# Chunk 2's normed rows take another way into the MLP, in a newly ordered DeltaNet + MLP kernel

## The chip, the cores and the metric

The kernel runs on one core of a Trainium2 chip. The metric is the device time of one execution in microseconds (us). The core has five engines that each run their own instruction stream in order: TensorE (PE; PEld is its weight load), VectorE (DVE), ScalarE (ACT), GpSimd (POOL) and SyncE (SP), which only issues DMAs here. Engines wait for each other by semaphores.

## The reference

A DeltaNet attention over 4 batches, 8 heads, 768 positions and head size 48 is followed by an MLP block on the rows of 8 x 48 = 384 values:

```python
for t in range(S):
    y[:, :, t] = einsum('bhd,bhde->bhe', q[:, :, t], state)
    v_old = einsum('bhde,bhd->bhe', state, k_n[:, :, t])
    state = state + beta_t * einsum('bhd,bhe->bhde', k_n[:, :, t], v[:, :, t] - v_old)
x = y as (B, S, H*D)
xn = (x - mean) / sqrt(var + 1e-6) * g_ln
out = x + relu(xn @ w_ch1) @ w_ch2          # 384 -> 1536 -> 384
```

Keys are divided by their norm first. All of it is float32.

## The kernel before

The 768 positions are cut into 12 chunks of 64. A chunk holds 4 x 64 = 256 rows for the MLP. The names c0 to c11 stand for the recurrence of a chunk (`recur`, from L1020) and m0 to m11 for its MLP (`mlp`, from L1420).

For a chunk's recurrence the kernel needs a Gram matrix of its keys (`gram`, stored to DRAM in `gds`), the inverse of a triangular matrix made from it, products with queries and state, and the state's update. From chunk 2 on the inverse is made for two chunks together: `rows_inverse` (L864) loads blocks of the Gram matrices from DRAM, eliminates column by column on VectorE (L906 and L913, 31 columns) and stores the result to DRAM, from where it is loaded back as blocks (`xq`). `join` (L964) joins the blocks on TensorE.

At the end of `recur` stands the path of the rows into the MLP, which the change touches. ScalarE copies the attention's output to `x` (L1164). VectorE takes mean and variance (L1170, L1171), ScalarE the root (L1176), VectorE the normed rows `xln`, one instruction of 128 rows for each of two row groups (L1182). The MLP needs them turned, with the 384 channels on partitions, scaled by `g_ln`: the tile `xnt`. There are two ways to it, and the constant `LNPE` chooses by the chunk's number:

- `c <= LNPE`: for each row group TensorE turns three blocks of 128 x 128 into a PSUM bank (L1216, tile `by`, or `two` in chunk 0), and ScalarE (or VectorE, L1221) scales them into `xnt`, 128 columns at a time (L1231).
- `c > LNPE`: VectorE turns blocks of 32 x 32 into `xlt` (L1193, one instruction a row group), SyncE stores `xlt` to the DRAM tile `xld` (L1198) and loads it back with four DMAs, one for each 32 partitions (L1201), and ScalarE scales three times 256 columns (L1208). In this way the columns of `xnt` come in another order, which alternates blocks of 32 rows of the two row groups.

The MLP of chunks 0 to 2 is written out plainly: 12 tiles of the first layer (L1438 for chunk 0, L1458 for chunks 1 and 2), a ReLU on ScalarE (L1446, L1467). From chunk 3 on (`FROM`) the first layer is `fifteen`, which makes it from sums of blocks (L1339; it needs the columns alternated). The second layer is plain in chunk 0 (L1480) and `seven` from chunk 1 on (L1555), with 42 products of 128 x 192. In chunks 1 and 2 the ReLU writes `h_all` with the two row groups apart:

```python
h_all[:, hk] if c <= LNPE else h_all[:, hk].rearrange("p (g i b) -> p i g b", g=2, b=BK),
p[:, 0:TOK] if c <= LNPE else p[:, 0:TOK].rearrange("p (i g b) -> p i g b", g=2, b=BK), ACTF.Relu,
```

The order of the work is written out by hand. Every function only records steps (`Line.add`): an engine, a closure that issues one or several instructions, and what it reads and writes. The string `ORDER` (L131 to L242) lists all steps by number, and `Line.emit` issues them in that order; `in_this_order` then holds every engine to it, so that an engine's stream is the listed steps of that engine, one after the other. SyncE's DMAs stand in the same list: one that waits for its data holds up those behind it. The letter f stands for a filler, a product of zeros on TensorE (L1633) that keeps it busy. They stand in the first 60 us, where chunk 0's inverse is made by a chain of short steps on TensorE, VectorE and ScalarE (`first_inverse`).

Weights arrive as pairs of 32-bit words and are put together by ScalarE, VectorE and GpSimd (`convert`) in the first 110 us, from DMAs that ScalarE issues.

Of the kernel before, what the change touches and what calls it, by code (L numbers as in the profile page):

```python
# [131 lines left out]
52 59 57 54 58 56 8 10 9 11 5 12-13 2 0 65 15 14 41 49 254 66 43 7 19 23 1 45 47 46 48 53 55 6 39 72 37-38 76 71 69 89  # L132
96 f 79-80 f f 85-86 81-82 105-106 88 90-91 87 103-104 17 31 16 20 97 92-93 83 74 98 84 107 99 73 70 75 40 108 213 26
18 35 21-22 100-101 94 34 102 95 24 124-125 118 219 211 78 128 f f f f 109-110 f f f 220 126 29 119 32 120 111 122 112
129 77 123 121 225 127 223 241 113 63-64 67 261 312 263 260 259 256 258 262 257 323 313 408 405 68 311 310 f 130 132
131 133 f f 140 134 f f 224 141-142 135-136 215 143 138-139 137 145 235 221 144 245 229 227 212 247 243 253 226 42 61
f f f 146 f f 147 4 f 148 150 114 149 156 f 152 242 25 33 28 151 246 f 155 161 154 153 f f f 115 162 f 659 62 60 658
44 661 f 157 236 27 158 163 166-167 116-117 159-160 244 248 360 164 206 f f 264 171 169-170 f 265 30 165 228 266 36
267 168 3 268 255 269-273 50 216 172 178 361 175-176 233 177 231 217 51 179 f f f 207 182 174 173 274-277 184 278 183
208 214 367 237 187 185-186 180 f f 325 403 398 324 322 238 663 181 209 279-280 f 314 316 366 194 188 281 195 282  # L140
189-190 362 240 283 232 284-298 363 299-300 f 315 317 198 193 199 239 201 318-319 200 191-192 f 320 f f f 368 210 196
326-327 334 197 202 364 335 338 329 203 249 204 328 340 342-343 205 251 346 671 230 234 218 670 664-665 222 369
347-348 f f f 330 336 f 352 f 331-332 355 353-354 673 250 252 672 365 674 662 660 572 337 339 358 573 341 344-345
349-351 574 576 407 409 402 321 410 301 406 399 356-357 304-306 411 333 400 309 303 302 308 307 472 474 471 473 404
359 432 431 788 401 415 575 370 578 598 434 433 579 412 577 435 580-581 675 470 413 582 584 599 372 585 604 373 605
583 475 588 610 586 611 587 416 378 589 379 616 592 617 417 593 596-597 635 418 590 636 591 594 666 436 371 414 437
602 374 384 595 600 382 603 376 608 601 609 385 790-792 794 793 787 789 784 476-479 481 677 482-499 419-420 500-502
480 375 503-504 439 421 1075-1076 676 377 614 422 424 615 606 425 391 423 607 380 390 620 438 426 430 427 429 428 386
505-507 678 508-513 1087 381 514-524 383 1088 621-623 612 440-441 637 624 638 392 442 394 388 443 445 447 446 613 387
795 525 393 444 389 395 1086 396-397 1089-1090 1077 639 625 667 450 448 668 526 650 527-534 449 535-537 626-627  # L150
679-680 452 451 453 538-539 628 640 796 651 454 641 629 618 630 656 652 455-457 653-654 540 657 541-544 458 642 631
462 459-460 465 619 463 643-647 797 632 921 785 1181 929 922-924 669 930 681 931 684 683 686 685 786 1079 682 1078 655
545 1183 648-649 933 926 549 546-547 464 461 826-827 687-691 693-708 548 634 928 1180 934-935 932 830 832 828 833 831
838 836 798 839 837 842 829 843 834 844 835 845 799 850 853 851 1091 1074 468 1081 1093 852 857 854 466 1080 467 1092
800 709-714 550 692 715-722 551 723-724 561 725 936 726-730 859-863 554 552-553 555-560 840 864 801 841 865 802 876
846 867 856 866 805 807 806 803 562 877 848 878-879 810 808 811 809 804 847 564 815 812 563 813 816 731 849 565 817
822 814 818 825 566 821 819-820 823 869-873 824 927 567 570 569 568 571 732 1082 733-740 937 940-941 938 942 939 1553
1098 883 855 880 886-887 881 888-889 874 943 858 868 469 1555 1186 1188-1189 1187 925 1190 1371 633 1179 1191 944 1369
1178 1370 741 875 742-745 890-891 746-756 892 894-899 757 945-946 1185 1661 1374 1192 947 882 948 901-903 1083 893 885
949 951-952 1084 955 1094 1184 1554 884 1375 904 979 905-907 900 980 977 909 974 1565 1095-1096 950 953 956 985 981  # L160
1193 954 986 982 958 912-914 1194 915-917 975 959-960 976 1197 962 918 1198 971 1003 978 972-973 908 1085 758 760 1097
761 759 1102 1100-1101 1099 991 983 987 1377 1182 1378 1195 762 957 961 763 992 984 764-765 767 1103 988 766 997 989
768 990 1004 1006 1567 1556-1557 773 1196 769-771 998 772 995 993 1200 1012 994 996 1001 1104-1107 1109-1121 1199 1201
1002 1202 1013 1022 1014 999-1000 1015-1017 1023 1203 774 920 1379 910 919 963 1380 964 1373 966 1381 967 911 1376 965
1853 1007 1005 1010 1008-1009 1569 1552 1558 1011 1021 1568 1019-1020 1559 1564 1018 1029 1024-1025 1030 1039-1042
1031 1043 1032 1026-1027 1044 1033 1566 1037 970 969 968 1383 1852 1382 1036 1243 1236 1122-1139 1045 1028 1140-1141
1034 1046 1228 1038 1232 1054 1229-1230 1233 1247 1047-1052 1035 1204 1560 1053 1384 1205 1055-1059 775 778 777 1207
1206 1208-1209 1142 1210-1211 1385 776 779 782 1215 783 1212 781 780 1388 1060 1065-1069 1240 1070 1237 1231 1386 1389
1216 1143 1387 1390 1144 1213 1145 1217 1214 1146-1148 1391-1392 1238 1241 1248-1249 2045 1571 1570 1251 1255 1234
1071 1218 1149 1219 1393 1239 1252 1244 1253 1245 1254 1246 1256 1242 1150-1151 1250 1372 1855 1854 1656 1660 1664  # L170
1658 1657 1666 1663 1072 1665 1667 1220 1668 1062 1279 1270 1221 1224 1669 1223 1073 1222 1394 1267 1257 1264 1268
1265 1258 1572 1395 1108 1266 1561 1235 1289 1271 1284 1061 1259 1269 1152-1153 1275 1154-1161 1562 1272-1273 1276
1274 1277 1260 1280 1162-1163 1278 1573-1574 1281 1285 1261 1290 1286 1291 1164 1282 1165-1168 1292 1563 1063 1670
1169-1172 2152 1575 1064 1173 1283 1227 1293 1317 1396 1294-1295 1262 1318-1319 1296 1307-1309 1320 1310 1226 1225
1263 1297 1311-1312 1287 1313 1288 1321-1322 1324-1325 2047 2057 1577 1579 1578 1176 1580 1177 1174 1671 1326-1329
1323 1330 1298 1419 1299 1301 1304 1300 1302 1426 1305 1314-1315 1430 1303 1306 1316 1334-1336 1423 1342-1344 1420
1337-1339 1175 1851 1858 1850 1860 2150 1859 2153 1345-1346 1340 1349 1347-1348 1350-1352 1331 1360 1421 1353 1662
1332 1341 1581-1583 1398 1397 1584-1585 2058 1576 1587 1462 1333 1588 1424 1438 1354-1355 1357 1586 1401 1399-1400
1361-1362 1427-1428 1363-1365 1439 1434 1356 2044 1672-1673 1422 1403 1366 1589 1431 1435-1436 1425 1590-1595 1402
1596 1674 1429 1675-1676 1437 1677 1432 1440-1441 2059 1472 1453-1454 1467 2046 2049 2048 2056 2051 2061 1678 1597  # L180
1433 1442 1598 1447-1448 1450 1455 1680 1406 1682 1679 1681 1449 1683 1451 1456 1443-1444 1458 1407 1599-1602 1404
1603 1405 1604-1605 1684 1452 1606 1445 1686 1457 1459-1460 1463-1464 1468 1473-1474 1465 1461 1466 1469 1685 1408
1475 1687 1409 1476 1490-1491 1477-1478 1689 1856 1688 1410 1690 1481-1482 1484 2050 1483 1488 1470 1446 1471
1492-1495 1500-1503 1498 1607 1479-1480 1485 1487 1497 1608-1609 1504-1505 1359 1610 1486 1489 1499 1691 1496 1862
1857 1861 1863 1368 1659 1358 1506 1864 1411 1367 1414 1611-1613 1507-1510 1525 1511-1513 1614-1615 1866 1517-1522
1526 1523 1616-1617 1694 1692 1514 1524 1413 1412 1415 1417 1695 1618 2052 1619-1620 1693 2148-2149 2151 2345 1418
1416 1532-1534 1527-1531 1535-1536 1696 1717 1515 1724 2060 1718 1867 1728 1516 1697-1700 1865 2155-2156 2158
1543-1546 1537 1621-1625 1869 1868 1870-1872 1874 1547 1873 1876 1704 1701 1875 1548 1721 1719 1722 1538 1626
1725-1726 1627-1629 1705-1706 1630 1702 1720 1727 2062 1736 1732 2063 1737 1760 1877 1723 1549 1631 1880 1878 1708
# [56 lines left out]
def kernel(  # L246
# [18 lines left out]
    DFF = w_ch1.shape[1]  # L265
    KC = DM // 128
    FT = DFF // 128
    GH = 2 * H
    NP = H // 2
    TURNED = 4  # L270
    LNPE = 2
    GP = 2 * NP
    FROM, LATER = 3, 6
    JOINT = 3
    TOK = 256
    WN = 768

# [1504 lines left out]
```

## Time and profile before

| | us |
|---|---|
| median of 3 runs | 515.05 |
| lowest and highest | 513.08, 516.33 |
| profiled execution, its own time | 514.4 |
| its span | 512.7 |
| busy: TensorE | 499.4 |
| VectorE | 355.0 |
| GpSimd | 281.7 |
| ScalarE | 208.0 |

The span runs from the first to the last instruction of the profile; 1.7 us of the execution lie around it. Busy time is the union of an engine's instructions; an engine that is not busy waits or has nothing to do. TensorE's matmuls are pipelined, so rows that follow each other overlap a little, and each float32 product shows as two rows. The granted clock of TensorE is 0.997 on the mean. The chain of work that ended last is read from the end: at each step to what released the instruction, or to the one before it on its engine.

### The profile page before, as it was taken

The page shows a single profiled execution, that of the slowest core. Times are in us where ns is not written, and L with a number is a line of the kernel's source. Part 1 is how long each engine was busy: PE and PEld are TensorE (multiplying, and loading weights), DVE is VectorE, ACT ScalarE, POOL GpSimd, SP SyncE. Part 2 cuts the span into 40 slices and gives each one's busy share as a digit, 9 for nine tenths or more (in the row PEclk, how much of TensorE's full clock was granted, in tenths as well). Part 3 has the DMA queues.
Part 4 walks back from the last instruction along what each step waited for, and adds up shares of the span by engine and source line. Part 5 has one row for each costly group of instructions (what it writes and reads, how often), then busy time and mean ns, then how long its engine had stood idle before and what let it go on. Part 6 is the DMA issues. An engine that isn't in the chain of part 4 may idle for free.

```text
span 512.7 us, 21868 instructions
## 1 busy us (share of the span) xinstructions
PE 499.4 (97%) x9490; PEld 455.4 (89%) x9490; DVE 355.0 (69%) x843; ACT 208.0 (41%) x462; POOL 281.7 (55%) x447
## 2 busy tenths in 40 slices
PE   7998998999999999999999999999999999999997
PEld 5786897668898889899999999999999999999996
DVE  5677469698896798984989957998935555353241
ACT  4877644532443342251435243424323424324140
POOL 5442872344667879749574456264282732745554
PEclk9999899999999999999999999999999999999999
DMA  8979685578339756387433483442472303012011
GB/s 202 266 145 217 119 180 123 115 176 168 43 56 217 151 98 106 67 214 125 88 90 55 92 219 60 102 72 50 99 138 39 91 3 95 3 40 54 2 40 31
DMA packets 181631, 54.49 MB, mean 106 GB/s; under 512 B 164888, under 2 KB 177312, under 8 KB 181536
## 3 DMA queue, kind: packets, MB, share of 16 engines
q1 hardware_dynamic: 168512, 40.10, 37.7%
q10 hardware_dynamic: 10816, 9.83, 6.9%
q0 software_dynamic: 2208, 3.17, 4.2%
q8 instruction: 74, 1.21, 1.0%
q14 instruction: 21, 0.17, 0.1%
HBM read 36.30 MB, written 16.78 MB: 104 GB/s over the span
## 4 chain that ended last, share of the span: by engine, by line
PE 90%; DVE 4%; issue 2%; DMA 2%; ACT 1%; SPq 1%; POOL 0%; POOLq 0%; DVEq 0%; ACTq 0%
PE f L1555 28%; PE f L1339 23%; PE f L1458 6%; PE f L1633 4%; PE f L1480 3%; PE f L1438 3%; PE by L1031 2%; PE two L818 2%; PE two L1047 2%; PE by L1126 2%; PE two L1119 2%; PE two L1136 2%; DMA words<-in_moe_w_ch_dram 1%; PE by L980 1%; PE f L616 1%
## 5 line engine op out<-in xcount | busy, mean ns | idle before, releaser
L1542 POOL TENSOR_TENSOR h_all<-h_all 128x256 f32<-128x256 f32 x99 | 72.2, 741 | 18.7 <-DVE qt L913 4.6
L1555 PE MATMUL f<-w_sb,h_all 128*128 128x192 f32 x396 | 80.8, 331 | 0.0
L1555 PE MATMUL f<-words,h_all 128*128 128x192 f32 x396 | 75.8, 328 | 0.0
L1580 POOL TENSOR_TENSOR words<-h_all 128x128 f32<-128x128 f32 x66 | 30.0, 474 | 66.3 <-ACT h_all L1366 51.1
L1555 PEld LDWEIGHTS f<-w_sb,h_all 128*128 128x128 f32 x396 | 64.4, 190 | 1.8 <-DVE o L1573 0.2
L1362 DVE TENSOR_TENSOR h_all<-f,h_all 128x512 f32<-128x512 f32 x72 | 48.7, 684 | 24.7 <-PE f L1339 17.1
L1555 PEld LDWEIGHTS f<-words,h_all 128*128 128x128 f32 x396 | 64.9, 190 | 0.7
L906 DVE TENSOR_TENSOR tmp<-xb,gb 128x31 f32<-128x31 f32 (+19 forms) x139 | 52.4, 377 | 4.0 <-POOL xb L893 0.4
L1357 ACT COPY h_all<-f 128x512 f32<-128x512 f32 x45 | 26.0, 585 | 67.0 <-PE f L1339 60.7
L913 DVE TENSOR_TENSOR xb<-xb,tmp 128x31 f32<-128x31 f32 (+19 forms) x139 | 49.0, 352 | 3.3
L400 POOL DMA_DIRECT2D tb<-in_k_dram x64 | 42.2, 663 | 9.4 <-DMA ksum<-gd 9.1
L1366 ACT ACTIVATE h_all<-h_all 128x512 f32<-128x512 f32 x54 | 32.4, 626 | 28.3 <-DVE h_all L1362 28.1
L1339 PE MATMUL f<-xnt,w_sb 128*128 128x128 f32 x288 | 41.2, 279 | 0.0
L1339 PE MATMUL f<-x_new,w_sb 128*128 128x128 f32 x288 | 39.8, 277 | 0.0
L1339 PEld LDWEIGHTS f<-xnt,w_sb 128*128 128x128 f32 x288 | 36.9, 191 | 0.7
L1339 PEld LDWEIGHTS f<-x_new,w_sb 128*128 128x128 f32 x288 | 36.4, 192 | 0.7 <-DVE h_all L1362 0.2
L1573 DVE TENSOR_TENSOR o<-f,x 128x192 f32<-128x192 f32 x33 | 11.5, 351 | 33.5 <-PE f L1555 28.6
L1164 ACT COPY x<-by 128x384 f32<-128x384 f32 x23 | 10.5, 481 | 57.2 <-DVE o L1573 32.8
L1458 PE MATMUL f<-xnt,w_sb 128*128 128x256 f32 x144 | 33.6, 383 | 0.0
L1458 PEld LDWEIGHTS f<-xnt,w_sb 128*128 128x128 f32 x144 | 26.8, 190 | 3.6
L1633 PE MATMUL f<-u 128*128 128x256 f32 x94 | 26.1, 411 | 2.8 <-DVE xb L448 2.8
L681 POOL TENSOR_TENSOR v<-v,kpair 128x768 f32<-128x768 f32 x10 | 14.9, 1486 | 23.5 <-DVE xln L1182 13.7
(259 smaller groups left out, 1048.2 us busy)
## 6 DMA issues: line engine op xcount, KB each, us to landing
words<-in_moe_w_ch_dram ACTq DMA_DIRECT2D x20, 384.0 KB, 6.2
gd<-gsb SPq DMA_DIRECT2D x11, 512.0 KB, 4.4
v<-in_v_dram SPq DMA_DIRECT2D x24, 192.0 KB, 4.4
kr<-in_k_dram SPq DMA_DIRECT2D x46, 96.0 KB, 3.6
out_dram<-o SPq DMA_DIRECT2D x46, 96.0 KB, 2.4
xld<-xlt SPq DMA_DIRECT2D x9, 384.0 KB, 3.6
xnt<-xld SPq DMA_DIRECT2D x36, 96.0 KB, 2.8
tb<-in_q_dram SPq DMA_DIRECT2D x40, 64.0 KB, 3.0
```

The lines of the kernel that those rows point to most:

```text
L400: add(eng, cost, lambda: QUEUE[eng].dma_start(out=out_, in_=in_), r, w, bulk=n * ns / 16e3, np=n, **kw)
L906: lambda j=j, n=n, w=w, t=t: nc.vector.tensor_tensor(out=t, in0=xv[:, 0:n, j : j + 1].to_broadcast([128, n, w]), in1=gv[:, j : j + 1, j + ...
L913: "DVE", dve(n * w), lambda t=t, rest=rest: nc.vector.tensor_tensor(out=rest, in0=rest, in1=t, op=ALU.subtract),
L1339: nc.tensor.matmul(wide(p[:, f : f + 128]), w[:, f : f + 128], r, start=start and i == 0, stop=True, skip_group_check=True)
L1357: add("ACT", act(512), lambda: nc.scalar.copy(o, p), pk, ok)
L1362: add("DVE", dve(512), lambda: nc.vector.tensor_tensor(out=o, in0=x, in1=y, op=op), [*xk_, *yk], ok)
L1366: add("ACT", act(512), lambda: nc.scalar.activation(o, o, ACTF.Relu, scale=scale), [], ok)
L1458: nc.tensor.matmul(p[:, 0:TOK], w1_sb[:, t, f * 128 : (f + 1) * 128], xnt[:, t], start=(t == 0), stop=(t == KC - 1))
L1542: add(eng, cost, lambda: e.tensor_tensor(out=out_, in0=x, in1=y, op=op), r, w, port=2 if eng == "Pool" else 1, pr=-2)
L1555: lambda f=f, t=start and f == order[0]: nc.tensor.matmul(p[:, 0:D2], lhs(f), rhs[:, f], start=t, stop=(f == order[-1]), skip_group_check=True
L1580: lambda f=f + i: e.tensor_tensor(out=s3[f], in0=one(0, 0)[0](f), in1=one(1, 0)[0](f), op=ALU.subtract),
L1633: nc.tensor.matmul(f_[0][:, 256:512], nought, nought[:, 0:1].to_broadcast([128, 256]))
```

## The change

`LNPE` goes from 2 to 1, so chunk 2 takes the way through VectorE and DRAM that chunks 3 to 11 take. And `ORDER` is a new list, found by a search for this version.

```diff
 ORDER = """
-52 59 57 54 58 56 8 10 9 11 5 12-13 2 0 65 15 14 41 49 254 66 43 7 19 23 1 45 47 46 48 53 55 6 39 72 37-38 76 71 69 89
-96 f 79-80 f f 85-86 81-82 105-106 88 90-91 87 103-104 17 31 16 20 97 92-93 83 74 98 84 107 99 73 70 75 40 108 213 26
...
+57 54 56 52 58-59 10-13 25 3 1 5 66 49 65 7 15 28 19 17 22 16 18 29 32 23 30 26 31 33 50 35 34 20 36 2 21 27 24 255 8
+61 9 51 0 14 45 41 47 53 55 6 69 37-38 72 96 89 71 90 f 79-80 f 86 82 f 85 81 4 84 76 91-93 97 94 88 73 87 74 98-99
...
@@
-    LNPE = 2
+    LNPE = 1
```

Out go two steps of TensorE (three turns each) and six of ScalarE; in come two of VectorE, five DMAs of SyncE and three steps of ScalarE. All other 3,094 steps and fillers stay. Their numbers shift by what was put in, so the two lists can't be compared by number. Step by step, TensorE's steps stand 2.8 places from their old ones on the mean and 16 at most, VectorE's 3.8 and 71, ScalarE's 3.4 and 44, GpSimd's 3.5 and 41, SyncE's 6.8 and 69. The 47 fillers are still 47. VectorE's largest moves are at the very start: it now makes all masks, pads and the unit blocks first, and then begins on chunk 0's keys; GpSimd clears a tile that waits for the masks before it makes the identity that TensorE's turns use.

## The prediction

> **What bounds the kernel now.** I read the page first: busy shares, then the chain that ended last.
>
> ```profile
> PE 499.4 (97%) x9490; PEld 455.4 (89%) x9490; DVE 355.0 (69%) x843; ACT 208.0 (41%) x462; POOL 281.7 (55%) x447
> ...
> PE 90%; DVE 4%; issue 2%; DMA 2%; ACT 1%; SPq 1%; POOL 0%; POOLq 0%; DVEq 0%; ACTq 0%
> ```
>
> TensorE is busy 97% of the span and is 90% of the chain, so a microsecond taken off TensorE is one off the end, unless a wait takes its place. That is an average, so next the table by stage (columns: span, then busy time and instruction count of each engine, granted clock, DMA share, GB/s).
>
> ```profile
> 46.00:52.00 6.00, 3.95 (x66) 3.05 (x55) 3.80 (x16) 4.15 (x9) 0.00 (x0) 1.00 1.15 278
> 52.00:54.00 2.00, 2.00 (x77) 1.92 (x76) 0.56 (x1) 0.66 (x2) 1.58 (x3) 0.57 0.80 174
> 54.00:57.00 3.00, 3.00 (x57) 2.38 (x57) 0.51 (x1) 2.93 (x7) 3.00 (x5) 0.72 0.44 54
> 80.00:100.00 20.00, 17.88 (x460) 13.88 (x462) 17.01 (x37) 12.01 (x24) 5.04 (x4) 1.00 0.45 104
> 100.00:140.00 40.00, 40.00 (x862) 31.59 (x862) 34.41 (x85) 13.48 (x37) 20.80 (x29) 1.00 0.67 132
> 140.00:160.00 20.00, 20.00 (x623) 18.46 (x613) 18.19 (x48) 7.99 (x23) 11.56 (x15) 1.00 0.50 101
> 160.00:200.00 40.00, 40.00 (x735) 35.41 (x735) 31.86 (x65) 14.66 (x36) 32.82 (x44) 1.00 0.71 141
> ```
>
> From 100 us on TensorE has no hole, and chunk 2 (140 to 160) lies in that stretch. VectorE is nearly full there too: 18.19 of 20. The holes are in the first 100 us: 2.05 between 46 and 52, 2.12 between 80 and 100. The first of them in the chain in order of time (start, duration, what):
>
> ```profile
> 48.19 0.50 PE by L770 x23
> 48.69 2.05 issue
> 50.74 0.35 PE by L770 x9
> ```
>
> TensorE stops in the middle of one step's matmuls and waits for nothing that the profile names, while the DMA share is 1.15; I take it for a late fetch of its instructions. Just after, the granted clock is 0.57 for 2 us and 0.72 for 3: (1 - 0.57) x 2 + (1 - 0.72) x 3 = 1.70 us lost. Such a hole costs 2.05 + 1.70 = 3.75 us.
>
> **What goes.** Two turns on TensorE, three instructions of two passes each (in order of time: start, duration, engine, line, out<-in):
>
> ```profile
> 143.49 0.82 PE L1216 MATMUL by<-ident,xln 128*128 128x128 f32 x6
> ...
> 144.14 1.79 PE L1555 MATMUL f<-words,h_all 128*128 128x192 f32 x10
> ...
> 145.13 1.40 ACT L1231 ACTIVATE xnt<-by,g_sb 128x128 f32<-128x128 f32 x5
> ...
> 146.54 0.31 PE L1047 MATMUL two<-qs,kt 48*64 48x112 f32 x1
> ```
>
> The row's ends are modelled; the next product starts 144.14 - 143.49 = 0.65 us later, so 0.65 us of TensorE goes (0.11 an instruction), on the path.
>
> "TensorE: Matmul & The Clock Gate" of the Trainium skill, section "PE-mode transpose", gives some 275 ns for a turn of 128x128 in a kernel; by it the six would give 6 x 0.275 = 1.65 us, and the end 1 us less than I forecast. The trace has 0.11 us for the distance of one from the next, and that is what a pipelined engine gives back; the sum goes by it.
>
> Also gone: six scalings on ScalarE, 6 x 0.37 = 2.2 us. They read bank `by`, and the next user of `by`, chunk 3's product at L1047, starts at 146.54, just as the last ends (145.13 + 1.40). Its predecessor on TensorE also runs until then, so there was no wait to win, but the product may now come earlier. What is late next is VectorE, which reads that product. I count nothing.
>
> **What comes.** Chunks 3 to 11 already take this path, so the rows exist:
>
> ```profile
> L1193 DVE STREAM_TRANSPOSE xlt<-xln x18: 552/569/578, 169.6 to 457.7; 128x384 f32<-128x384 f32 x18
> ...
> L1208 ACT ACTIVATE xnt<-xnt,g_sb x27: 492/493/512, 189.9 to 471.0; 128x256 f32<-128x256 f32 x27
> ...
> L400 SPq DMA_DIRECT2D xnt<-xld x36: 557/622/1532, 180.3 to 463.8; - x36
> L400 SPq DMA_DIRECT2D xld<-xlt x9: 344/350/1476, 176.4 to 458.2; - x9
> ...
> DMA to landing us min/median/max: 2.5/2.9/4.5
> ```
>
> *VectorE*, 2 x 0.57 = 1.14 us more between 140 and 160, where it has 1.81 idle. Behind the turns stand chunk 6's key turn and the last third of the inverse of chunks 4 and 5, which ended at 157.06. Its store lands some 4 us later, and the loads of its blocks still stand behind the store of chunk 7's Gram matrix in SyncE's queue (issued at 164.45, as it needs TensorE's product). So 1.1 us later costs nothing there; if that store came early, 1.1 us of TensorE's wait for the join at 173.8 would be the price.
>
> *ScalarE*: 3 x 0.49 = 1.5 us for 2.2. The ReLUs of chunk 2 now write blocks of 32; 0.38 us each before, unknown for this form. L1208 itself takes 0.49 for as many elements, so between 0 and 12 x 0.11 = 1.3 us on an engine busy 8 of 20: nothing, and 1.3 if TensorE waited for each bank.
>
> *SyncE*: five issues, 0.35 + 4 x 0.62 = 2.8 us. In the new order the store stands behind three loads of chunk 4 whose waits end by 138; the four loads have one more chunk-4 load among them. So chunk 4's queries come some 3 us later in the queue than their place; their last two still issue near 160 behind the inverse's store, as before, and their product at 167.0 has that cover.
>
> *The path of the rows.* The last normed row was done at 143.66; in the new order one step of 0.41 moves ahead of it: 144.1. Turns 1.14: 145.2. Store to landing, a store's 3.6 at the median: 148.8. Four more issue places of 0.65: 151.4. Landing 2.9: 154.3. Three scalings 1.3: 155.6. In the new order chunk 2's first product stands after the same TensorE work, less 0.65 and plus two products of 0.325 taken ahead of it: 160.15, as before. So chunk 1's second layer covers the detour with 4.5 us to spare. With 4.5 us for each landing it is 145.2 + 4.5 + 2.6 + 4.5 + 1.3 = 158.1, still covered by 2 us.
>
> **The new order** moves every engine's steps, not chunk 2's alone. TensorE has the same 47 filler products and the same steps otherwise, moved by 2.8 places on the mean. I looked at each place of the kind product, reader on another engine, next product that needs the reader: TensorE's work between the two products, less the reader's duration, is under 0.4 us at 15 places after 100 us, at 17 before. So the new order plans no waits in. At the start VectorE now builds all masks first (some 30 short steps, about 5 us by their distances of 0.1 to 0.27) and fills the 4.16 us that it sat idle until 8.46; the key squares on ScalarE start at about 7.8 against 7.90. From below nothing is gained there, as the first 55 us are a chain with fillers. From above one step of 1.59 us, as one mask step took at 2.70 beside GpSimd, would put the start back by as much. I take 0.
>
> **Sum**: 514.4 (the profiled execution; span 512.7) - 0.65 = 513.75. That execution lies 0.65 under the median of the runs, 515.05; against it the sum is 514.4. I say 514.0. One per cent, 5.1 us, is about what a measurement of this kernel tells from no change.
>
> **The rivals.**
>
> 1. *A hole in the first 100 us closes*, because the masks leave VectorE's critical stretch and the weights' fetches move on ScalarE's queue. For it: 46 to 52 is the densest DMA stretch. Against: the steps and the number of instructions there are the same. Without the hole at 48.69: 514.0 - 3.75 = 510.2; without the 1.09 us at 95.91 too, 509.1.
>
> 2. *Slower: TensorE runs out of fetched instructions more often.* Place: the runs of 64 small products (chunk 3's, at 146 to 157, x623 in 20 us), which now meet chunk 2's store and loads. The price is 2.05 us and, from a hole of about 2 us on, 1.70 for the clock. Two such holes: 514.0 + 7.5 = 521.5. For it: 48.69, and 0.7 to 1.1 us at 86.3 and 95.9. Against: no hole in 140 to 200.
> The Trainium skill, "TensorE: Matmul & The Clock Gate", section "Why this matters for your kernels", asks for gaps of over some 3 us before the clock falls. By it two holes would cost 4.1 us and the end be 518.1. The trace shows the clock fall behind a hole of 2.05 us, so the sum keeps 3.75 each.
>
> 3. *The rows come late*, cover gone: the point is a landing over 2 us longer than any in the rows above. Each further microsecond is one on the end; at 3, 517.0. Against it: nine chunks of the same path.
>
> 4. *The change doesn't do what it says*: TensorE gets no shorter, as the 0.65 turns into small waits at the regrouped products: 514.4 to 515.05.
>
> **How the numbers follow.** Forecast 0.50, its own range 511.5 to 517; rival 1 0.20, half of it beyond 1%; rival 2 0.20, all beyond 1%; rival 3 0.07; rival 4 0.03. So faster by over 1%: 0.10, slower 0.20, within 1%: 0.70. The range goes from 509.5 to 521.5, and leaves out half of rival 1 and half of rival 2.
>
> **What would show it.** In the profile of the changed kernel no row L1216 stands after 115 us; VectorE has 20 turns at L1193, the first near 145; the scalings end near 156 and chunk 2's first product starts near 160 with no wait for ScalarE; TensorE is busy some 0.65 us less. I am wrong if a wait for `xnt` stands before that product, if holes over 1 us stand after 100 us, or if chunk 0's first product of the MLP (L1438, 60.1) moves by more than 2 us.

## The result and the profile after

| | before | after |
|---|---|---|
| median of 7 runs, us | 515.05 | 510.59 |
| lowest and highest | 513.08, 517.08 | 508.87, 512.80 |
| profiled execution, own time | 514.35 | 511.17 |
| its span | 512.7 | 509.5 |

The ratio is 0.9918, interval 0.9893 to 0.9944: 4.2 us less (2.9 to 5.5). The forecast was 514.0, 1 us less. In the changed kernel every line below `ORDER` has a number higher by one (L1193 is now L1194).

The busy shares and the chain's shares, from the page of the changed kernel:

```profile
PE 497.5 (98%) x9484; PEld 454.5 (89%) x9484; DVE 359.0 (70%) x845; ACT 209.2 (41%) x459; POOL 282.3 (55%) x447
...
PE 90%; DVE 4%; ACT 2%; issue 1%; DMA 1%; SPq 0%; ACTq 0%; POOL 0%; DVEq 0%; POOLq 0%
```

TensorE still sets the end; "issue", time without a named releaser, is 1% of the chain in place of 2%. The table by stage, for the same stretches as before (span, busy time and count of PE, PEld, DVE, ACT, POOL, then clock, DMA share, GB/s):

```profile
46.00:52.00 6.00, 4.86 (x139) 3.95 (x140) 4.64 (x22) 5.52 (x12) 0.91 (x2) 1.00 1.18 238
52.00:54.00 2.00, 1.87 (x72) 1.56 (x69) 1.18 (x2) 1.19 (x3) 1.48 (x3) 1.00 1.08 323
54.00:57.00 3.00, 2.43 (x94) 1.91 (x96) 1.25 (x5) 2.68 (x5) 2.99 (x5) 1.00 0.74 133
80.00:100.00 20.00, 18.56 (x586) 14.30 (x587) 16.29 (x34) 10.29 (x22) 8.87 (x8) 1.00 0.31 81
100.00:140.00 40.00, 40.00 (x825) 31.98 (x818) 36.76 (x92) 15.29 (x41) 16.27 (x24) 1.00 0.66 132
140.00:160.00 20.00, 19.58 (x535) 17.59 (x538) 17.23 (x45) 5.78 (x13) 12.68 (x17) 1.00 0.65 141
```

The clock stays at 1.00 between 52 and 57, where it was 0.57 and 0.72. The hole stands in the same product, behind the same 23rd instruction, but is 1.13 us long, not 2.05 (chain in order of time: start, duration, what):

```profile
49.78 0.50 PE by L771 x23
50.28 1.13 issue
51.40 0.35 PE by L771 x9
```

Where did 3.2 us between the two profiled executions go? From 20 us on, the view of TensorE's waits sums to 4.4 us without a releaser before and 3.0 after, and 2.1 and 1.7 with one. The half clock cost 1.7 before and nothing after, and 0.65 of turns is gone: 1.4 + 0.4 + 1.7 + 0.65 = 4.15 less. Up to 20 us of work the new kernel is 0.7 behind. That makes 3.45, within 0.3 of the 3.18 measured. Setting both traces side by side at equal TensorE work (an estimate, each row of TensorE taken at its usual distance to the next), the new kernel is 0.7 us behind at 27 us, some 1.5 at 45, level at 62, 1.6 ahead at 81 and 3.0 at 100; at the end it is 2.9 ahead, and the turns come on top. So in these two executions all but the turns is won between 45 and 100 us, where no step of the edited path stands.

The path itself went as worked out, only earlier (rows by line with first and last start; the last two are chunk 2's alone):

```profile
L1194 DVE STREAM_TRANSPOSE xlt<-xln x20: 535/570/580, 141.3 to 453.9; 128x384 f32<-128x384 f32 x20
...
L1209 ACT ACTIVATE xnt<-xnt,g_sb x3: 496/497/512, 151.1 to 151.9; 128x256 f32<-128x256 f32 x3
L1459 PE MATMUL f<-xnt,w_sb x6: 379/379/483, 158.1 to 159.3; 128*128 128x256 f32 x6
```

The turns start at 141.3 (the forecast had 144.1 to 145.2), the scalings end at 152.4, and the first product of chunk 2's MLP starts at 158.1 without a wait: a cover of 5.7 us.

### The profile page after: what moved, and what is told of

Same layout as the page of the kernel before. It is cut to its first block, busy times and chain, and to the rows that moved or that the text cites. A ratio compares the mean times of both kernels' runs of the same rounds, so it can differ in the third digit from the quotient of the medians.

```text
span 509.5 us, 21842 instructions
## 1 busy us (share of the span) xinstructions
PE 497.5 (98%) x9484; PEld 454.5 (89%) x9484; DVE 359.0 (70%) x845; ACT 209.2 (41%) x459; POOL 282.3 (55%) x447
## 4 chain that ended last, share of the span: by engine, by line
PE 90%; DVE 4%; ACT 2%; issue 1%; DMA 1%; SPq 0%; ACTq 0%; POOL 0%; DVEq 0%; POOLq 0%
PE f L1556 29%; PE f L1340 23%; PE f L1459 6%; PE f L1439 3%; PE f L1481 3%; PE f L1634 3%; PE by L1127 2%; PE by L1032 2%; PE two L819 2%; PE two L1120 2%; PE two L1048 2%; PE two L1137 2%; PE by L987 1%; PE f L617 1%; PE by L981 1%
## 5 line engine op out<-in xcount | busy, mean ns | idle before, releaser
L1556 PE MATMUL f<-words,h_all 128*128 128x192 f32 x396 | 78.4, 330 | 0.0
L914 DVE TENSOR_TENSOR xb<-xb,tmp 128x31 f32<-128x31 f32 (+19 forms) x139 | 51.8, 373 | 3.3
L1340 PE MATMUL f<-x_new,w_sb 128*128 128x128 f32 x288 | 41.2, 278 | 0.0
L1556 PE MATMUL f<-w_sb,words 128*128 128x192 f32 x132 | 25.9, 330 | 0.0
```

The lines of the kernel that those rows point to most:

```text
L914: "DVE", dve(n * w), lambda t=t, rest=rest: nc.vector.tensor_tensor(out=rest, in0=rest, in1=t, op=ALU.subtract),
L1340: nc.tensor.matmul(wide(p[:, f : f + 128]), w[:, f : f + 128], r, start=start and i == 0, stop=True, skip_group_check=True)
L1556: lambda f=f, t=start and f == order[0]: nc.tensor.matmul(p[:, 0:D2], lhs(f), rhs[:, f], start=t, stop=(f == order[-1]), skip_group_check=True
```

## The experiments

The first four take the change apart. `ORDER` can be mixed: all steps that the old list has up to some step form a set that needs nothing outside it, so this set can stand in the order of one list and the rest in the order of the other.

**The path alone.** The new path in the old order.

```diff
-    LNPE = 2
+    LNPE = 1
 ORDER, old numbers:
-822 818
...
-819-821 823-825
 ORDER, new numbers:
+818-819
...
+820 824 821-822
...
+823
...
+827 825-826
```

In old numbers 818 and 822 are the turns on TensorE and the rest the scalings. In new ones 818 and 819 are VectorE's turns, 820 the store, 821 to 824 the loads, 825 to 827 the scalings.

> The old order of steps, with chunk 2's rows on the new path and nothing else moved: its two turns on TensorE and six scalings are gone, its VectorE turns, its store, four loads and three scalings are put in where the new order has them in relation to their neighbours on the same engine. Theory A (the path is worth only its TensorE time; what the new kernel gains beyond it comes from the first 100 us of the new order): 0.65 us less than the kernel before, 514.4 against 515.05. Theory B (the path itself frees something later, the bank, ScalarE or VectorE's queue, that is worth the 4.5 us of the whole change): 510.5 to 511. Theory C (the rows come late without an order made for them): 515 to 517, with a wait for the scaled rows ahead of chunk 2's first product. In the profile, the late fetches at 50.7, 87 and 97 us should still be there.

Measured: 517.25 (ratio 1.0034, 1.0008 to 1.0060), 1.8 us slower than before, and not 0.65 faster. The chain of this kernel shows the price (start, duration, what):

```profile
145.69 0.54 DVE xlt L1193
...
152.85 0.57 DVE v L1058
153.41 0.04 issue
153.46 1.15 PE by L1031 x64
```

TensorE waits 1.75 us for chunk 3's values `v`, which VectorE makes a dozen steps behind the two turns. Less the 0.65 of turns this makes 1.1 us slower, within the interval (0.4 to 3.1). The medians, 517.25 and 514.82 on the same chip, are 2.4 apart. Half clock cost 2.6 us a run here and 1.5 before (one less the mean granted clock, times the span; the mean of the runs, without the longest one, 522.81), which is about the rest. That the wait brings it about was not shown: in the profiled execution the clock fell at 98 us, ahead of it.

The profile of before had the warning (VectorE's step for `v` in chunk 3, and TensorE's product behind it):

```profile
150.01 0.55 DVE L1058 TENSOR_TENSOR v<-v,by 128x384 f32<-128x384 f32 x1
...
150.85 1.15 PE L1031 MATMUL by<-qs 48*64 48x48 f32 x64
```

`v` was done at 150.56 and TensorE took it 0.3 us later, without a wait: that was the slack of this step, though VectorE was idle 1.81 us in that stretch as a whole. With the turns, `v` comes 1.4 us later behind the step at L1146 that VectorE does ahead of them (10.41 us from its start to the end of `v`, 9.05 before), and TensorE arrives 0.65 earlier; less the 0.3 of slack that is the 1.75 of waiting.

**The early order alone** and **the late order with the path.** The first 643 steps, to about 100 us, in the one order, the rest in the other.

```diff
 ORDER (early order alone: these 643 steps, then the old list):
-52 59 57 54 58 56 8 10 9 11 5 12-13 2 0 65 15 14 41 49 254 66 43 7 19 23 1 45 47 46 48 53 55 6 39 72 37-38 76 71 69 89
+57 54 56 52 58-59 10-13 25 3 1 5 66 49 65 7 15 28 19 17 22 16 18 29 32 23 30 26 31 33 50 35 34 20 36 2 21 27 24 255 8
...
```

> The old path of chunk 2's rows. All steps that the old list has up to TensorE's last product of chunk 0's second layer but a few (643 of 3102, up to about 100 us) stand in the new order, all steps after them in the old one. Theory A: nearly the whole gain without the path's 0.65, so 4.5 - 0.65 = 3.8 us at the medians, 3.2 - 0.65 = 2.6 by the two profiled executions: 511.2 to 512.4; no fall of the granted clock behind 51 us, holes ahead of TensorE up to 100 us about 3 us in sum in place of 5.3. Theory B: 514.5 to 515.5.

> The new path of chunk 2's rows. The same 643 steps up to about 100 us stand in the old order, all steps after them in the new one. Theory A: 0.65 us less than before, 514.4, with the holes of the old kernel at 50.7, 87 and 97 us and the half clock behind the first. If the new order gains after 100 us: 510.5 to 512.

Measured: early order alone 512.05 (0.9944, 0.9922 to 0.9965), 2.9 us less. Path with the late order 514.08 (0.9990, 0.9967 to 1.0012), 0.5 us less, which is the 0.65 within the interval. The two sum to 3.4, the whole change to 4.2 (2.9 to 5.5). And the late order is no bystander: it takes the path from 1.8 us slower to 0.5 faster, 514.08 against 517.25 in runs on the same chip. In it VectorE makes chunk 3's `v` two column pairs of the inverse sooner, done at 151.83 for 153.41, and TensorE's wait for it is gone. The late order with the old path was not run, so what it is worth by itself isn't shown; the three waits of the kernel before that stand behind 100 us sum to 0.8 us.

**The early order from 45 us on.** As the early order alone, with the old order kept up to TensorE's product at 44.9 us.

```diff
 ORDER (347 old steps stay; the next 296 in the new order, from here):
-318-319 200 191-192 f 320 f f f 368 210 196 326-327 334 197 202 364 335 338 329 203 249 204 328 340 342-343 205 251
+210 192 191 318-319 200 320 f f f f 196 326-327 334 197 202 364 368 335 338 329 328 249 340 342-343 251 346 204 230
...
```

> The old path of chunk 2's rows; old order up to TensorE's product at 44.4 us, new order for the other steps up to about 100 us, old order again after that. Theory A, sharpened: in the two profiled executions the new kernel is 1 us behind at 40 us and wins 1 us at the hole near 50 and 2.9 us from 60 to 98. So this mix keeps the old, faster start: 515.05 - 0.9 - 2.9 = 511.2, or 510.2 if the start's 1 us comes on top. If it is the placing of the weights' loads before 44 us that decides the hole near 50, it stays: 2 us of hole and 1.7 of clock are back, 513 to 514.

Measured: 511.66 (0.9925, 0.9899 to 0.9952), 3.9 us less. The masks and the start bring nothing that the intervals could show; the gain is made by the 296 steps between 45 and 100 us. Then each third of them by itself:

```diff
 ORDER (the second third, 84 steps):
-573 341 344-345 349-351 574 576 407 409 402 321 410 301 406 399 356-357 304-306 411 333 400 309 303 302 308 307 472
...
+400 411 402 573 370 341 344-345 359 576 349 577 574 409 407 410 321 301 406 309 306-307 401 302 333 305 304 308 404
...
 ORDER (the last third, 144 steps):
-590 636 591 594 666 436 371 414 437 602 374 384 595 600 382 603 376 608 601 609 385 790-792 794 793 787 789 784
...
+666 590-591 594 436 371 397 414 376 602 385 595 382 374 600 603 384 437 608 636 601 380 609 614-615 790 789 792-793
...
```

> The old path and the old order, but the 68 steps of the list that stand between TensorE's products at 44.9 and 61.5 us are in the new order. What the early order gains (2.9 us in one run, 3.2 to 3.9 in another, less 0.5 of clock) lies in one of three stretches. If it is this one (the hole in the product at 50.7 us and the half clock behind it): 512 to 513. If it lies later: 514.5 to 515.5, with the hole at 50.7 still there.

> The same with the 84 steps between TensorE's products at 61.5 and 79.7 us. In the kernel before, TensorE waits there for ScalarE's ReLUs twice, at 76.2 and 77.6 us, 0.53 + 0.72 = 1.25 us beyond its pace, in every run that has the old order there, and in none that has the new one. If such hand-offs count: 1.25 us less, 513.7. If only late instructions count: no change, 514.5 to 515.3.

> The same with the 144 steps between 79.7 and 100 us. In the kernel before there are three holes without a releaser here, 0.32 + 0.72 + 1.09 = 2.1 us, and no other wait. If the new order spreads the small products so that instructions come in time: 513 to 513.5. If these holes only move: 514.5 to 515.3.

| steps in the new order | median, us | ratio (interval) | us against before |
|---|---|---|---|
| 44.9 to 61.5 us | 515.27 | 0.9995 (0.9972 to 1.0018) | -0.3 |
| 61.5 to 79.7 us | 514.21 | 0.9976 (0.9946 to 1.0007) | -1.2 |
| 79.7 to 100 us | 513.08 | 0.9956 (0.9936 to 0.9976) | -2.3 |

The thirds sum to 3.8, as the 3.9 of all three. The most lies in the last one, the only third whose interval excludes no change. The hole near 50 us isn't it, as far as one profile and the median tell: in the profile of the first third it is gone, but a hole of 1.36 us stands at 92.3 us and half clock behind it, and the median hasn't moved.

The second third agrees with its 1.25 us, but isn't shown by its interval. Its two waits stand in this view of the kernel before, which counts 0.9 us of them (1.25 by the distances of the rows' starts). All eight profiled kernels with the old order there have them, and none of the six with the new one (TensorE's waits, 60 to 79 us):

```profile
PE f L1480 <- ACT h_all L1446: 0.5, 1, 0.5
...
PE f L1438 <- ACT h_all L1446: 0.4, 1, 0.4
```

The old order has a first-layer product right behind another one on the same bank, and a second-layer product right behind the ReLU that feeds it. The new one puts another product between. But with the old start a new wait appears (chain of the kernel with this third alone):

```profile
66.97 6.45 DMA gb<-gd
73.42 0.02 issue
73.44 0.26 ACT nrm_b L882
```

A load that takes 6.45 us holds ScalarE's queue, the ReLU behind it, and TensorE for 1.7 us. The other two kernels with the old start and this third in the new order wait there for 1.4 us; those with the new start don't.

**What the holes are.** One kernel leaves every step in its place and renumbers TensorE's stream.

```diff
+    small_ones = []
+
     def zeros():
         nc.tensor.matmul(f_[0][:, 256:512], nought, nought[:, 0:1].to_broadcast([128, 256]))
+        while len(small_ones) < 32:
+            small_ones.append(nc.tensor.matmul(f_[0][0:32, 256:257], nought[0:32, 0:32], nought[0:32, 0:1]))
 
     line.filler = (zeros, 0.44, "f0")
-    for _ in range(3):
-        fill(1, 512, f_[3], FK[3], pr=-100)
+    for n in (64, 64, 512):
+        fill(1, n, f_[3], FK[3], pr=-100)
```

> The old kernel, with 32 products of 32x32x1 on zeros put behind the first filler product, so that all later TensorE instructions have a number higher by 128 in its stream (a product of this type makes four rows, two loads and two multiplications); two of the three start products of 512 columns are cut to 64 to make room. They add to no result. If holes without a releaser come from the stream (TensorE is out of instructions each time that 256 more have run): they again stand at a number of 193 or 194 modulo 256, so none is left in the L770 product behind its 23rd instruction; one may stand 128 instructions earlier or later. If they belong to the place (this product, this moment of dense transfers): the 2 us hole stays behind the 23rd instruction of that product, now at a number of 65 modulo 256. The time: 513 to 517, as the holes fall elsewhere.

Measured: 524.28 (1.0193, 1.0150 to 1.0236), where the kernel before had 514.94 on that chip: 9.3 us slower. The 32 products ran one after another and took 3.57 us, so the start is 2.4 us later (the same product at 12.39 and 14.76 us); the other 7 us come later. The profiled execution is the longest of the four, 528.7. In it the waits without a releaser sum to 11.1 us from 20 us on, in place of 4.4, and two of them lie where the kernel before has none (150.7 and 172.0 us, 1.7 and 1.2). The longest, in the chain:

```profile
48.87 0.74 PE f L818 x32
49.60 3.72 issue
53.32 1.13 PE f L818 x20
```

That L770 product now runs through. The new hole stands at row 1986 of TensorE's stream (loads, products and its sequencer's rows counted), the old one stood at 1985: another instruction, the same number. Over all fourteen profiled executions the 56 longest holes without a releaser stand at a number of 193 or 194 modulo 256; of the 61 waits of 0.3 us or more with a releaser, three do. The page has the counterpart, a queue of 74 transfers of 16 KB for some 19,100 rows, one for 256:

```profile
q8 instruction: 74, 1.21, 1.0%
```

So TensorE stops where a block of 256 instructions ends and the next has not come. The trace times it: the fetch ahead of the 2.05 us hole started 3.6 us behind the block's start, while the data transfers' share was 1.15; ahead of the blocks from 57 to 90 us it starts 1.1 to 1.7 behind. It took 1.39, and TensorE went on 1.45 after its end. "Runtime: NRT & Kernel Launch" of the Trainium skill, section "Instruction fetch mechanics", says that instructions come in blocks of 256 and that crossing into the next is mostly hidden. The blocks agree with these runs; the crossing is hidden only where the fetch ends early enough. Over all block borders of the fourteen executions TensorE never went on sooner than 1.2 us after the end of the fetch, and behind the holes it went on 1.2 to 1.9 after it.

From these times I took some 4 us as the least that a block must last and summed what each block of both streams lacks. That forecast a size:

```diff
+        while len(small_ones) < 4:
+            small_ones.append(nc.tensor.matmul(f_[0][0:32, 256:257], nought[0:32, 0:32], nought[0:32, 0:1]))
...
-    for _ in range(3):
-        fill(1, 512, f_[3], FK[3], pr=-100)
+    for n in (448, 512, 512):
+        fill(1, n, f_[3], FK[3], pr=-100)
```

> The old kernel with four products of 32x32x1 on zeros behind the first filler (16 rows on TensorE) and one start product cut from 512 to 448 columns: every later TensorE instruction has a number higher by 16 in the stream, else nothing changes. If the holes follow blocks of 256 instructions, and a block that takes under some 4.0 to 4.2 us costs what it lacks, the blocks of the old stream lack 2.9 to 4.5 us behind 40 us as they are, and 1.7 to 3.1 when shifted by 16: 1.2 to 1.4 us less, 513.7. If the blocks don't matter: 515.

> The changed kernel with the same edit. Its blocks lack 1.8 to 3.4 us as they are, 4.1 to 5.5 when shifted by 16: 2.1 to 2.3 us more, 512.8, a ratio to the kernel before of 0.996 in place of 0.992. So with 16 more rows ahead of both, the change would be worth some 1 us in place of 4.5. If the blocks don't matter: 510.6, 0.992.

Measured: the old kernel 514.01 (1.0004, 0.9984 to 1.0025), where -1.2 was expected: a miss. The new one 512.02 (0.9953, 0.9931 to 0.9975), 1.8 us worse in its ratio than unshifted, as expected, though the intervals overlap. (The start moved by 0.2 us or less in both.) With 16 more rows ahead of both, the change is worth 2.0 us at the medians of this chip, in place of 4.2: part of its gain may hang on where the blocks end. The sum of lacking blocks tells a shift by half a block from none, but not one by 16, as no length of a block decides: in the profiled executions blocks of 2.7 to 2.9 us passed without a hole, where the fetch started 0.2 to 0.5 behind the block's start, and blocks of over 5 us ended in one, where it started 2.5 to 5.2 behind. How late a fetch starts differs from one execution to the next. The shift by 128 also starts the kernel 2.4 us later against its transfers, and no run tells how much of the 7 us comes from that.

**Which step of VectorE should wait?** The path alone, with three column pairs of the inverse put behind chunk 3's five steps, about as in the new order.

```diff
-734-740 939 942-943 940 944 941 1555 1100
+734 939 942-943 940 944 941 735-740 1555 1100
```

> The old order with the new path for chunk 2's rows (the kernel that was 1.8 us slower than before), and one more edit on VectorE: three pairs of steps of the inverse of chunks 4 and 5 (1.2 us a pair... 2.4 us in all, six steps of 0.4) stand behind chunk 3's five steps on its values and products, not ahead of them, as they do in the new order. If the path's loss is VectorE's 1.1 us of turns, which stand ahead of chunk 3's values for which TensorE then waits 1.75 us at 153.5: that wait goes, and the time falls by 1.75 us or more, to 515.4 or less, at best to before less 0.65 (514.3). If the loss comes from the store, the loads or the scalings, the time stays at 516.5 to 517.

Measured: 518.74 (1.0090, 1.0064 to 1.0115), 4.6 us slower than before: a miss. The wait for `v` is gone, and a longer one has come (TensorE's waits, then the chain):

```profile
PE f L1555 <- POOL h_all L1542: 5.1, 1, 5.1
```

```profile
152.50 0.13 POOL xb L871
152.63 0.78 issue
153.41 0.91 POOL h_all L1542
```

GpSimd's step at L871 waits for the last of these three pairs, now done at 152.44, and behind it in GpSimd's queue stand the sums of `h_all` that TensorE's second layer of chunk 1 needs. In the new order these sums stand ahead of that step. So VectorE's 1.1 us of turns can't be pushed from one customer to the next; GpSimd's order has to change with it.

**Old start, all else new.**

```diff
 ORDER (347 old steps, then the new list):
-57 54 56 52 58-59 10-13 25 3 1 5 66 49 65 7 15 28 19 17 22 16 18 29 32 23 30 26 31 33 50 35 34 20 36 2 21 27 24 255 8
+52 59 57 54 58 56 8 10 9 11 5 12-13 2 0 65 15 14 41 49 254 66 43 7 19 23 1 45 47 46 48 53 55 6 39 72 37-38 76 71 69 89
...
```

> The changed kernel, but with the old order up to TensorE's product at 44.9 us (347 of the steps). From the parts: 0.5 us less for path and late order, 3.9 less for the order from 44.9 to 100 us: 510.6, the same as the changed kernel. If the old start's 1 us at 38 us (in the two profiled executions) is real: 509.6.

Measured: 510.86 (0.9936, 0.9913 to 0.9959), 3.3 us less than the kernel before on that chip (513.86; 2.1 to 4.5 less), where the parts said 4.4: no better than the changed kernel. The new start's lag in one trace is worth nothing that the medians show.

## Why the prediction's range held and its ground did not

The time, 510.59, lies inside the stated range of 509.5 to 521.5, but below the forecast's own part of it, 511.5 to 517: it came from the part that rival 1 put there. The mechanism that was forecast, 0.65 us of turns and all else nothing, was not the one at work. That the path and its late order together come to 0.5 is partly luck: two terms that the sum has at nothing, 1.75 us of waiting for `v` and the order that takes it away, cancel.

- **TensorE bounds, holes only in the first 100 us**: right. Behind 100 us the changed kernel has no hole of over 0.3 us.
- **0.65 us of turns**: right, as far as it can be told; path and late order together measure -0.5 (-1.7 to 0.6). (A turn is one row and not two passes, six rows of 0.27 us that start 0.11 apart; the sum isn't touched by it.)
- **What would show it**: no turn of rows on TensorE behind 115 us, 20 turns on VectorE, and chunk 0's first product of the MLP at 60.1 in both traces: as forecast. TensorE's busy time fell by 1.9 us, not 0.65, as time at half clock counts as busy too.
- **The rows' path, cover 4.5 us**: right; 5.7, no wait for the scaled rows. The ReLU's new form takes 0.38 us a tile, as the old one, so its bound of 1.3 us was nothing. SyncE's five issues delayed nothing that TensorE waited for.
- **VectorE's 1.14 us at nothing, as it "has 1.81 idle"**: this step failed in its reason. Idle time in a stretch of 20 us is not slack of a step. The turns stand ahead of chunk 3's `v`, which was done only 0.3 us before TensorE took it. In the old order they cost 1.75 us of waiting, more than the 0.65 that TensorE saves. I named the key turn and the inverse as what stands behind them and missed `v` and, through the inverse, GpSimd.
- **"The new order: I take 0"**: this step failed. I compared tight hand-offs behind 100 us only, 15 for 17, though the holes and the waits for ReLUs stood ahead of 100 us. The order is worth 2.9 us there (1.8 to 4.0 by one run, 2.5 to 5.2 by another), and 2.3 more behind it, of which 1.75 is the wait for `v`.
- **Rival 1**, 510.2 at a chance of 0.20: the time that came, 510.59. Its place was half right: in the profiled execution the 2.05 us hole shrank to 1.13 and the clock stayed up, but with the medians the gain is in the last third, 80 to 100 us. Its reason, masks and fetches of weights, fell: the start brings nothing.
- **Rival 2**, fetches late behind 140 us: didn't happen to this change, but the mechanism is real. The shift by 128 made it happen at 150.7 and 172.0 us.
- **Rivals 3 and 4**: no. The path alone was slower by another mechanism than late rows.

What stays open: why the last third gains 2.3 us. In the profile of before it has three holes of 2.1 us in all, with this third reordered none; but over the executions profiled, holes in this stretch sum to 0.7 to 2.1 with the old order and 0 to 1.5 with the new one. Fewer falls of the clock make 0.7 of it (0.47 us a run lost to half clock, 1.15 in the kernel before); the rest isn't settled.

## What to carry to other kernels

An engine's idle time in a stretch says nothing of a step put into it: look at the engine's next steps whose results the bounding engine takes, and at how long before it takes them they are done. Here that was 0.3 us. Judge a new order where the waits and holes are, not where the edit is. And in a long unrolled program on TensorE, the number of instructions ahead of a dense stretch is itself a parameter: try a shift before explaining a change of a per cent by what was edited.

## What the runs showed of the hardware

- TensorE can stand for 0.2 to 3.7 us at every 256th instruction, where the fetch of the next block ends late: it went on no sooner than 1.2 us after the fetch's end, and ahead of the holes a fetch took 0.9 to 1.8 us. 128 rows of no work at the start moved the kernel by 1.9%, a quarter of it their own time.
- Inside the kernel the half clock lasts 3.41 us or, in two executions, twice that, and the other records' lengths are multiples of it too (44.37 is 13 times, 92.16 is 27 times 3.413): the clock is set window by window. The seven windows with 1.88 to 2.80 us of TensorE idle were all followed by one at half clock; of 36 with 0.8 to 1.7 idle, five were. A hole cut by a window's border can cost less than one inside it: one of 2.33 us that ended at 25.95, in the kernel with three column pairs put back, left 1.70 in one window, and the clock stayed up. "TensorE: Matmul & The Clock Gate" of the Trainium skill, section "Part 1: The HAM clock gate", has such a window of some 3.4 us, and asks for an idle one before the clock falls; here a window a little over half idle was enough.
